# One fold over n and d before the split into even and odd, a fifth halved step in some blocks, and a first load in four pieces

## The chip, the cores and the metric

The kernel runs on one core of one Trainium2 chip. The metric is the device time of one execution in microseconds (us). TensorE (PE) multiplies matrices, PEld is its weight load, VectorE (DVE), ScalarE (ACT) and GpSimd (POOL) work elementwise, and SyncE (SP) only issues transfers here. POOL issues the loads, the transfers through the scratch tensor and the spread copies; SP issues the stores of the output.

## The reference

The input x is (8, 3008, 256), w_in (256, 2048), w_out (2048, 256), all float32.

```python
X = np.fft.fft(x, axis=1)
X = np.fft.fft(X, axis=2)
a = X.real.reshape(8 * 3008, 256)
h = np.maximum(a @ w_in, 0.0)
out = h * h @ w_out
```

Only the real part of the transform is used, so row k of a batch and row -k are linked, and x can be folded: what is needed of it are sums and differences of x(n,d), x(-n,-d), x(n,-d) and x(-n,d).

## The kernel before

**Transform.** The transform over d is multiplied into w_in once: `gh` holds three matrices (128 x 2048), cosine, sine, and -2 times the sine (`gh_turn`). The transform over n is done by TensorE on folded data. Per batch i, `load_x` loads x as fp16 into `t`, four quarters of six rows for each of 128 partitions: quarters 0 and 1 straight (`direct`), quarters 2 and 3 mirrored in n (`mirrored`, an indirect gather). There is one buffer for it, so the next load waits for the last reader of this one. `fold_steps(i)` then folds it on DVE:

- `d_even` (L389) sums d with -d into `fe`, `d_odd` (L396) takes their difference into `fo`, for all four quarters (24 rows of 128). `d_odd` also issues the next load of x.
- `n_cos` (L402) and `n_sin` (L405) combine a quarter with its mirrored one into `ab` (cosine and sine part, 12 rows of 130 each).
- `odds` (L412, or `odd` for one part) gives `od` for the odd rows of the output, `nyq` fills in its column 0 by two tiny matmuls, `even` (L422) gives `ev`, which goes to DRAM and comes back differently laid out (`back`) for the late fold (`late`: fold8, fold16, nyq8) of the even rows.
- `z_steps` multiplies `od` (unit (i, 0)) or the late fold's tiles (unit (i, 1)) with tables of cosines and sines; ACT evicts the first half of such a sum to `es` (L531) and the second to the columns zc, zs; DVE adds the mirrored half of the columns (`minus`, L542). Part 0 is zc, part 1 zs, and h is the half.

**Blocks.** The output columns are worked off in 25 blocks w (`wins`; widths 240, 512, 376, 376, 512, 448, then 512 and a last one of 360). A block goes through eight steps s of 256 hidden units each. A full step makes p+q by four matmuls into a PSUM tile `ph` (`pq`), lets ACT evict it with ReLU and DVE or ACT square it (`square`; steps in the second list of the plan have the first square done by ACT), turns it into p-q by two more (`turn`), and evicts and squares again. A halved step (`half_q`, `half_p`) makes q by two matmuls, evicts -2q to `sn` (L822), adds p by two more, evicts p+q to `hd` (L830), and leaves p-q, the ReLU and the square to DVE (`row_sum`: L838, L842; `halves`: L852, L853, L854), for one or two steps at a time. So a halved step has four ph matmuls where a full one has six, and more DVE work. `plan(w)` says which steps are halved; `PLAN` holds the lists.

Between the halves of each step `others(s)` puts the work of other kinds into the queues: the jobs `at[s]` of the folds, two of the 16 parts of the previous block's second matmul (L669, eight matmuls of 256 columns each, evicted by L684 and stored), the jobs `post[s]`, and from step `lo` on the z matmuls for the next block. The order of each engine's queue is the order in which this code runs (manual schedule). Both h2 (the squares) and `hd` have two buffers, h1 five, `ph` two. `row_spread` has POOL copy row 0 of zs to all partitions (`eb`) for L838.

Blocks by what they do besides: with the first part of a fold (`first_at`: 4, 7, 9, 11, 14, 17; d_even and n_cos), with its main part (`fold_at`: 5, 8, 10, 13, 16, 19; d_odd, n_sin, odds, nyq, even, back), with the late fold (`late_at`: 6, 9, 12, 15, 18, 21). Block 1 has the whole fold 1, block 2 the table for the even rows. Halved steps by block from 5 on: 4 5 5 4 3 4 5 5 4 5 5 4 5 5 4 6 5 6 6 5.

**Start.** Tables of cosines are made while x is loaded; `fold_steps(0)` runs by quarters (L578 to L590), then the first z matmuls, with `gh` made in between: `gh_step` (L475, both parts of 512 columns, one scaled by ACT, one by DVE) and `gh_half` (L486, one part, scaled by DVE). Block 0 has its own order (L891 to L917), four hidden chunks at a time (`pq4`, `turn4`, `square4`), with the last parts of `gh` between. `idle` issues matmuls whose result nobody reads.

## Time and profile before

| | |
|---|---|
| time, median of 3 runs | 595.66 us (595.61 to 595.82) |
| the profiled execution, its own time | 595.68 us |
| its span | 593.90 us |
| granted clock of TensorE | 1.00 |
| start to the first matmul of block 0 | 19.5 us |
| blocks 0 to 4 | 19.5 to 110.9 us |
| blocks 5 to 23 | 110.9 to 558.6 us |
| block 24 and the last second matmul | 558.6 to 593.9 us |

A busy share is the mean over all these stretches. Matmul rows overlap each other, so their busy time is an upper bound of what TensorE needs; the distance from one start to the next tells the pace. An arrow `<-` in a bracket names what ended the idle time before a row. First matmuls of some blocks (us from the start of the span): block 1 at 28.11, 2 at 48.43, 4 at 88.11, 5 at 110.88, 8 at 179.93, 9 at 203.56, 10 at 228.51, 11 at 252.55, 12 at 276.74, 13 at 299.66, 14 at 323.89.

### The profile page before, as it was taken

The page shows a single profiled execution, that of the slowest core. Times are in us where ns is not written, and L with a number is a line of the kernel's source. Part 1 is how long each engine was busy: PE and PEld are TensorE (multiplying, and loading weights), DVE is VectorE, ACT ScalarE, POOL GpSimd, SP SyncE. Part 2 cuts the span into 40 slices and gives each one's busy share as a digit, 9 for nine tenths or more (in the row PEclk, how much of TensorE's full clock was granted, in tenths as well). Part 3 has the DMA queues.
Part 4 walks back from the last instruction along what each step waited for, and adds up shares of the span by engine and source line. Part 5 has one row for each costly group of instructions (what it writes and reads, how often), then busy time and mean ns, then how long its engine had stood idle before and what let it go on. Part 6 is the DMA issues. An engine that isn't in the chain of part 4 may idle for free.

```text
span 593.9 us, 11346 instructions
## 1 busy us (share of the span) xinstructions
PE 574.7 (97%) x4352; PEld 418.4 (70%) x4352; DVE 533.8 (90%) x777; ACT 515.4 (87%) x665; POOL 109.9 (18%) x153
## 2 busy tenths in 40 slices
...
GB/s 147 206 119 138 54 87 36 80 132 102 51 56 106 120 87 86 118 114 59 40 116 104 111 41 46 115 125 92 49 36 68 70 100 43 53 51 46 63 58 68
DMA packets 37630, 50.42 MB, mean 85 GB/s; under 512 B 4583, under 2 KB 30743, under 8 KB 37575
## 3 DMA queue, kind: packets, MB, share of 16 engines
...
q1 hardware_dynamic: 26899, 24.44, 13.7%
q8 instruction: 34, 0.56, 0.4%
...
q14 instruction: 21, 0.17, 0.1%
...
## 4 chain that ended last, share of the span: by engine, by line
PE 66%; ACT 16%; DVE 9%; issue 6%; DMA 1%; ACTq 0%; POOL 0%; SPq 0%; DVEq 0%; POOLq 0%
PE po L669 39%; PE ph L828 7%; ACT h L799 7%; PE ph L814 6%; PE ph L789 4%; PE ph L790 4%; PE ph L795 4%; PE pz L526 3%; ACT sn L822 3%; ACT osb L684 2%; ACT hd L830 2%; DMA xo<-in_x_dram 1%; DVE hd L852 1%; ACT h L802 1%; DVE hd L853 1%
## 5 line engine op out<-in xcount | busy, mean ns | idle before, releaser
L669 PE MATMUL po<-wout,h 128*128 128x256 f16 (+1 forms) x3024 | 361.7, 273 | 0.0
L669 PEld LDWEIGHTS <-h 128*128 128x128 f16 (+1 forms) x3024 | 296.6, 98 | 71.2
L799 ACT ACTIVATE h<-ph 128x1024 f16<-128x1024 f32 (+3 forms) x172 | 164.3, 990 | 5.7 <-PE ph L790 3.3
L830 ACT ACTIVATE hd<-ph 128x1024 f16<-128x1024 f32 (+3 forms) x106 | 104.8, 990 | 26.2 <-PE ph L828 21.8
L854 DVE TENSOR_TENSOR h<-hd 128x4096 f16<-128x4096 f16 (+6 forms) x59 | 117.7, 1995 | 2.5
L822 ACT ACTIVATE sn<-ph 128x1024 f16<-128x1024 f32 (+3 forms) x106 | 104.6, 988 | 0.6 <-PE ph L814 0.6
L842 DVE TENSOR_TENSOR sn<-sn,hd 128x2048 f16<-128x2048 f16 (+6 forms) x59 | 63.5, 1076 | 16.3 <-ACT sn L822 12.0
L804 DVE TENSOR_TENSOR h<-h 128x1024 f16<-128x1024 f16 (+3 forms) x108 | 68.4, 668 | 8.6 <-ACT h L799 8.0
L852 DVE TENSOR_TENSOR hd<-hd,sn 128x2048 f16<-128x2048 f16 (+6 forms) x59 | 63.4, 1074 | 7.3 <-ACT hd L830 5.4
L684 ACT ACTIVATE osb<-po 128x512 f32<-128x512 f32 (+3 forms) x95 | 54.4, 576 | 15.7 <-PE po L669 14.9
L802 ACT ACTIVATE h<-h 128x1024 f16<-128x1024 f16 (+3 forms) x64 | 65.0, 1015 | 2.0
L828 PE MATMUL ph<-zc,gh 128*128 128x512 f16 (+3 forms) x212 | 61.0, 369 | 4.8 <-ACT sn L822 4.3
L853 DVE TENSOR_SCALAR hd<-hd 128x4096 f16<-128x4096 f16 (+6 forms) x59 | 63.7, 1080 | 1.6
L789 PE MATMUL ph<-zc,gh 128*128 128x512 f16 (+3 forms) x172 | 63.7, 371 | 0.6 <-ACT h L885 0.3
L790 PE MATMUL ph<-zs,gh 128*128 128x512 f16 (+3 forms) x172 | 63.7, 371 | 0.0
L838 DVE TENSOR_SCALAR hd<-eb,wv 128x512 f16<-128x512 f16 (+3 forms) x212 | 61.4, 346 | 2.5 <-DMA eb<-zs 2.5
L814 PE MATMUL ph<-zs,gh 128*128 128x512 f16 (+3 forms) x212 | 61.0, 370 | 0.0
L795 PE MATMUL ph<-zs,gh 128*128 128x512 f16 (+3 forms) x172 | 48.8, 370 | 0.2
...
L814 PEld LDWEIGHTS <-gh 128*128 128x128 f16 x212 | 20.6, 97 | 23.1
L790 PEld LDWEIGHTS <-gh 128*128 128x128 f16 x172 | 16.8, 98 | 19.0 <-issue 1.0
L789 PEld LDWEIGHTS <-gh 128*128 128x128 f16 x172 | 16.7, 97 | 18.1
...
## 6 DMA issues: line engine op xcount, KB each, us to landing
...
```

The lines of the kernel that those rows point to most:

```text
L669: nc.tensor.matmul(po[0:m, j * D : (j + 1) * D], h2[:, fc, q : q + m], wout16[:, fc, :], start=(fc == 0 and (j == 0 or not four or i > 3)) ...
L789: nc.tensor.matmul(ph[:, a, 0:wn], gh[:, 0, f0 : f0 + P], zcw[:, 0:wn], start=True, stop=False)
L790: nc.tensor.matmul(ph[:, a, 0:wn], gh[:, 1, f0 : f0 + P], zsw[:, 0:wn], start=False, stop=True)
L795: nc.tensor.matmul(phs[s][:, a, 0:wn], gh[:, 2, f0 : f0 + P], zsw[:, 0:wn], start=False, stop=True, skip_group_check=True)
L799: nc.scalar.activation(h1[:, :, 0:wn], phs[s][:, :, 0:wn], AF.Relu)
L802: nc.scalar.activation(h2[:, 2 * s : 2 * s + 2, 0:wn], hv, AF.Square)
L814: nc.tensor.matmul(ph[:, a, 0:wn], gh[:, 1, f0 : f0 + P], zsw[:, 0:wn], start=True, stop=True)
L822: nc.scalar.activation(sns[g][:, i : i + 2, 0:wn], ph[:, :, 0:wn], AF.Copy, bias=0.0, scale=-2.0)
L828: nc.tensor.matmul(ph[:, a, 0:wn], gh[:, 0, f0 : f0 + P], zcw[:, 0:wn], start=False, stop=True, skip_group_check=True)
L830: nc.scalar.activation(hds[g][:, i : i + 2, 0:wn], ph[:, :, 0:wn], AF.Copy, bias=0.0, scale=1.0)
L853: lambda: nc.vector.tensor_scalar(out=hv, in0=hv, scalar1=0.0, scalar2=None, op0=ALU.max),
L854: lambda: nc.vector.tensor_tensor(h2[:, 2 * g[0] : 2 * g[-1] + 2, 0 : 2 * wn], hv, hv, op=ALU.mult),
```

## The change

The fold starts with one sum over both signs, `cs` = x(n,d) + x(-n,-d) (`sums`, 12 rows of 255, column 0 apart into `ab`), from which `even_d` and `odd_d` make the cosine and sine part of `ab` by adding or subtracting the mirrored d (12 rows of 128). `fe` and `fo` go, `ab` is made once. The first part of a fold is now `sums` and `even_d`, the main part `load`, `odd_d` and the rest as before; block 1 has sums, then even_d and load, then odd_d.

The plan: main-fold blocks (5, 8, 10, 13, 16, 19) halve five steps (0 1, 3 4, 6) in place of four (1 2, 4 5); block 9 halves four in place of three; the others stay.

The first load comes as quarter 0, quarter 2, quarter 1, quarter 3, and the first fold works on quarters 0 and 2, then 1 and 3. `gh_step` is folded into `gh_half`; in block 0 the scalings of `gh` come ahead of the squares, whose DVE half `square4` now returns; `even` of fold 0 moves from block 0's step 7 to before block 0. In block 4 the z matmuls of unit (1,1) go part 0, part 1, part 0, part 1.

```diff
@@ -60,8 +60,8 @@
     PLAN = {
         6: (((0, 1), (2, 3), (4, 5)), (6, 7)),
         5: (((0, 1), (2, 3), (4,)), (5, 6, 7)),
+        "main": (((0, 1), (3, 4), (6,)), (2, 5, 7)),
         4: (((1, 2), (4, 5)), (0, 3, 6)),
-        3: (((1, 2), (4,)), (0, 5, 6)),
         "third": (((2, 3), (4, 5)), (0, 1, 6, 7)),
         "fourth": (((1, 2), (3, 4), (5,)), (0, 6, 7)),
         "fifth": (((2, 3),), ()),
@@ -146,10 +146,11 @@
         def mirrored(q):
             gather(q, idx["r" if q == 3 or b + 1 < B else "c"][:, 0:1], o + ((S if q == 2 else H) - R * (P - 1)) * D)
 
-        if b > 0:
+        if i == 0:
+            direct(0, 1)
+            yield t
+        elif b > 0:
             direct(0, 2)
-            if i == 0:
-                yield t
         else:
 
             gather(0, idx["f"][:, 0:1], o + D)
@@ -157,6 +158,8 @@
             direct(1, 2)
 
         mirrored(2)
+        if i == 0:
+            direct(1, 2)
         if b + 1 == B:
 
             nc.gpsimd.dma_start(
@@ -290,11 +293,10 @@
 
     spn = fop.tile([P, 2, 2, P], F16, name="spn")
     nc.vector.memset(spn, 0.0)
-    fe = fop.tile([P, 4, R, 130], F16, name="fe")
-    fo = fop.tile([P, 4, R, 130], F16, name="fo")
-    fo0 = fo.rearrange("p q c d -> p (q c) d")[:, :, 0:1]
-    nc.vector.memset(bass.AP(tensor=fo0.tensor, offset=fo0.offset, ap=list(fo0.ap[0:2]) + [[129, 2]]), 0.0)
-    nc.vector.memset(fe.rearrange("p q c d -> p (q c) d")[:, :, 129:130], 0.0)
+    cs = fop.tile([P, 2, R, D], F16, name="cs")
+    ab = fop.tile([P, 2, 2, R, 130], F16, name="ab")
+    nc.vector.memset(ab[:, 1, :, :, 0:1], 0.0)
+    nc.vector.memset(ab[:, :, :, :, 129:130], 0.0)
     turn2 = small([P, 1], "turn2")
     nc.vector.tensor_scalar(out=turn2, in0=dvec, scalar1=0.0, scalar2=2.0, op0=ALU.is_equal, op1=ALU.mult)
     nc.vector.tensor_scalar(out=turn2, in0=turn2, scalar1=-2.0, scalar2=None, op0=ALU.add)
@@ -377,33 +379,27 @@
 
     def fold_steps(i):
         t = xs.pop(i)
-        ab = fop.tile([P, 2, 2, R, 130], F16, name="ab", tag="ab")
         od = evp.tile([P, 2, R, 130], F16, name="od", tag="od")
         ev = fop.tile([P, R, 2, 130], F16, name="ev", tag="ev")
         folded[i, 0] = od
         st = {}
-        xf = t.rearrange("p q c d -> p (q c) d")
-        fef = fe.rearrange("p q c d -> p (q c) d")
-        fof = fo.rearrange("p q c d -> p (q c) d")
-
-        def d_even(a=0, b=4, eng=nc.vector):
-            r = slice(R * a, R * b)
-            if a < 3 <= b:
+
+        def sums(a=0, b=2, eng=nc.vector):
+            if a == 0:
                 nc.vector.tensor_copy(t[0:1, 2, 0, :], t[0:1, 0, R - 1, :])
-            eng.tensor_copy(fef[:, r, 0:1], xf[:, r, 0:1])
-            nc.vector.tensor_tensor(fef[:, r, 1:129], xf[:, r, 1:129], rev_dim(xf[:, r, 128:256], 2), op=ALU.add)
-
-        def d_odd(a=0, b=4):
-            r = slice(R * a, R * b)
-            nc.vector.tensor_tensor(fof[:, r, 1:129], xf[:, r, 1:129], rev_dim(xf[:, r, 128:256], 2), op=ALU.subtract)
-            if i + 1 < B and b == 4:
+            m = t[:, a + 2 : b + 2]
+            nc.vector.tensor_tensor(cs[:, a:b, :, 1:D], t[:, a:b, :, 1:D], rev_dim(rev_dim(m[:, :, :, 1:D], 2), 3), op=ALU.add)
+            eng.tensor_tensor(ab[:, 0, a:b, :, 0:1], t[:, a:b, :, 0:1], rev_dim(m[:, :, :, 0:1], 2), op=ALU.add)
+
+        def load():
+            if i + 1 < B:
                 xs[i + 1] = next(load_x(i + 1))
 
-        def n_cos(a=0, b=2):
-            nc.vector.tensor_tensor(ab[:, 0, a:b], fe[:, a:b], rev_dim(fe[:, a + 2 : b + 2], 2), op=ALU.add)
-
-        def n_sin(a=0, b=2):
-            nc.vector.tensor_tensor(ab[:, 1, a:b], fo[:, a:b], rev_dim(fo[:, a + 2 : b + 2], 2), op=ALU.subtract)
+        def even_d(a=0, b=2):
+            nc.vector.tensor_tensor(ab[:, 0, a:b, :, 1:129], cs[:, a:b, :, 1:129], rev_dim(cs[:, a:b, :, 128:256], 3), op=ALU.add)
+
+        def odd_d(a=0, b=2):
+            nc.vector.tensor_tensor(ab[:, 1, a:b, :, 1:129], cs[:, a:b, :, 1:129], rev_dim(cs[:, a:b, :, 128:256], 3), op=ALU.subtract)
 
         def odd(part):
 
@@ -468,28 +464,27 @@
             nc.gpsimd.tensor_copy(spn[:, 1, :, 0:1], yt[:, 0, 0, :, 128:129])
 
         late = [lambda: fold8(0), lambda: fold8(1), lambda: fold16(0), lambda: (fold16(1), nyq8())]
-        return {"d_even": d_even, "n_cos": n_cos, "odd": odd, "odds": odds, "d_odd": d_odd, "n_sin": n_sin, "nyq": nyq, "even": even, "back": back, "late": late}
+        return {"sums": sums, "load": load, "even_d": even_d, "odd_d": odd_d, "odd": odd, "odds": odds, "nyq": nyq, "even": even, "back": back, "late": late}
 
     gh = const.tile([P, 3, F], F16, name="gh")
 
-    def gh_step(cc):
+    def gh_half(cc, i, act=False):
         f0 = cc * 512
         fw = f0 % (F // 2)
-        pg = ps_h.tile([P, 2, 512], F32, name="pg", tag="psh")
-        for i, t in enumerate((c_all, s_n)):
-            for c in range(2):
-                nc.tensor.matmul(pg[:, i, :], t[:, c, 0:P], w16[f0 // (F // 2)][:, c, fw : fw + 512], start=(c == 0), stop=(c == 1))
-        nc.scalar.activation(gh[:, 0, f0 : f0 + 512], pg[:, 0, :], AF.Copy, bias=0.0, scale=1.0 / HS)
-        nc.vector.tensor_scalar(out=gh[:, 1, f0 : f0 + 512], in0=pg[:, 1, :], scalar1=1.0 / HS, scalar2=None, op0=ALU.mult)
-        gh_turn(cc)
-
-    def gh_half(cc, i):
-        f0 = cc * 512
-        fw = f0 % (F // 2)
-        pg = ps_o.tile([P, 512], F32, name="pg", tag="po")
+        if act:
+            pg = ps_h.tile([P, 2, 512], F32, name="pg", tag="psh")[:, 0, :]
+        else:
+            pg = ps_o.tile([P, 512], F32, name="pg", tag="po")
         for c in range(2):
             nc.tensor.matmul(pg, (c_all, s_n)[i][:, c, 0:P], w16[f0 // (F // 2)][:, c, fw : fw + 512], start=(c == 0), stop=(c == 1))
-        return lambda: nc.vector.tensor_scalar(out=gh[:, i, f0 : f0 + 512], in0=pg, scalar1=1.0 / HS, scalar2=None, op0=ALU.mult)
+
+        def scale():
+            if act:
+                nc.scalar.activation(gh[:, i, f0 : f0 + 512], pg, AF.Copy, bias=0.0, scale=1.0 / HS)
+            else:
+                nc.vector.tensor_scalar(out=gh[:, i, f0 : f0 + 512], in0=pg, scalar1=1.0 / HS, scalar2=None, op0=ALU.mult)
+
+        return scale
 
     def gh_turn(cc):
         f0 = cc * 512
@@ -575,29 +570,27 @@
 
     f0s = fold_steps(0)
     z0 = z_steps(need[0][0], late=True)
-    f0s["d_even"](0, 2, nc.gpsimd)
-    f0s["d_odd"](0, 2)
-    f0s["d_even"](2, 3, nc.gpsimd)
+    f0s["sums"](0, 1, nc.gpsimd)
+    f0s["even_d"](0, 1)
     nc.gpsimd.dma_start(out=wout16, in_=moe_w_out.rearrange("(c p) o -> p c o", p=P))
-    f0s["n_cos"](0, 1)
-    f0s["d_odd"](2, 3)
-    f0s["n_sin"](0, 1)
-    f0s["d_even"](3, 4, nc.gpsimd)
-    f0s["n_cos"](1, 2)
+    f0s["odd_d"](0, 1)
+    f0s["sums"](1, 2, nc.gpsimd)
+    f0s["load"]()
+    f0s["even_d"](1, 2)
     f0s["odd"](0)
-    f0s["d_odd"](3, 4)
-    f0s["n_sin"](1, 2)
+    f0s["odd_d"](1, 2)
     f0s["odd"](1)
     run(*z0(0, 0))
     idle(3)
     run(*z0(0, 1))
     f0s["nyq"]()
-    gh_step(0)
-    run(*z0(1, 0))
-    gh_step(1)
-    run(*z0(1, 1))
+    for h in range(2):
+        run(gh_half(h, 0, True), gh_half(h, 1))
+        gh_turn(h)
+        run(*z0(1, h))
     gh_half(2, 0)()
     run(*z0(0, 2), *z0(1, 2))
+    f0s["even"]()
     evec_i = iota([P, 2], [[1, 2]], 0, 2, "evec_i")
 
     evec = small([P, 2], "evec")
@@ -705,7 +698,7 @@
 
     def fold_jobs(i):
         f = folds[i] = fold_steps(i)
-        return [f["d_even"], f["n_cos"], f["d_odd"], f["n_sin"], f["odds"], f["nyq"], f["even"], f["back"]]
+        return [f["sums"], f["even_d"], f["load"], f["odd_d"], f["odds"], f["nyq"], f["even"], f["back"]]
 
     fold_at, late_at = {}, {}
     for i in range(2, B):
@@ -725,10 +718,11 @@
         if w < 5:
             return PLAN[("third", "fourth", "fifth")[w - 2]]
         first, late, main = w in first_at, w in late_at, w in fold_at
-        if w == 6 or late and not need[w + 1]:
-            return PLAN[5]
-        n = 4 if main or late else 5 if first or w + 1 == NW else 6
-        return PLAN[n - (first and late)]
+        if first and late:
+            return PLAN[4]
+        if main:
+            return PLAN["main"]
+        return PLAN[5 if first or late or w + 1 == NW else 6]
 
     def halved(w):
 
@@ -746,7 +740,7 @@
         at = [[] for _ in range(NST)]
         post = [[] for _ in range(NST)]
         if w == 0:
-            at[7] = [f0s["even"], f0s["back"]]
+            at[7] = [f0s["back"]]
         elif w == 1:
             fj = fold_jobs(1)
             at = [fj[0:1], fj[1:3], fj[3:4], fj[4:5], [], [], [], []]
@@ -778,7 +772,7 @@
         zj, zl = [], []
         for u in need[w + 1]:
             zu = z_steps(u)
-            zj += [(zu, p, h) for p, h in (((0, 0), (1, 0), (1, 1), (0, 1)) if lo == 4 else ((1, 0), (0, 0), (1, 1), (0, 1)))]
+            zj += [(zu, p, h) for p, h in (((0, 0), (1, 0), (0, 1), (1, 1)) if lo == 4 else ((1, 0), (0, 0), (1, 1), (0, 1)))]
         f2 = ffn2_steps(*old) if old else []
         phs = {}
 
@@ -885,32 +879,27 @@
             nc.scalar.activation(h1[:, :, 0 : 2 * wn], phs[s][:, :, 0 : 2 * wn], AF.Relu)
             hv = h1[:, :, 0 : 2 * wn].rearrange("p a (b n) -> p a b n", b=2)
             hv = rev_dim(hv, 3) if sg else hv
-            nc.vector.tensor_tensor(h2[:, 2 * s : 2 * s + 4, sg * wn : (sg + 1) * wn].rearrange("p (a b) n -> p a b n", b=2), hv, hv, op=ALU.mult)
+            return lambda: nc.vector.tensor_tensor(h2[:, 2 * s : 2 * s + 4, sg * wn : (sg + 1) * wn].rearrange("p (a b) n -> p a b n", b=2), hv, hv, op=ALU.mult)
 
         ng = 2 if w == 0 or wins[w - 1][1] < 384 < wn else 1
         if w == 0:
             pq4(0)
-            gh_half(2, 1)()
             pq4(2)
-            square4(0, 0)
-            gh_turn(2)
-            square4(2, 0)
+            g2 = gh_half(2, 1)
+            p0, p2 = square4(0, 0), square4(2, 0)
             turn4(0)
-            gh3 = [gh_half(3, 0)]
+            g3 = [gh_half(3, 0)]
             turn4(2)
-            gh3.append(gh_half(3, 1))
-            run(*gh3)
-            square4(0, 1)
-            square4(2, 1)
-            gh_turn(3)
+            g3.append(gh_half(3, 1))
+            m0, m2 = square4(0, 1), square4(2, 1)
+            run(g2, *g3, p0, lambda: gh_turn(2), p2, lambda: gh_turn(3), m0, m2)
             for s in (4, 6):
                 pq4(s)
-            for s in (4, 6):
-                square4(s, 0)
-            for s in (4, 6):
-                turn4(s)
-            for s in (4, 6):
-                square4(s, 1)
+            for sg in range(2):
+                for s in (4, 6):
+                    if sg:
+                        turn4(s)
+                run(*[square4(s, sg) for s in (4, 6)])
             for s in range(NST):
                 others(s)
             old = (w, h2)
```

## The prediction

> **What bounds the kernel now.** I read the page's busy times first, then the timeline for the pace of TensorE, then the busy time by stretch, one stretch per column block, and last the DVE rows of the fold and the places where TensorE waits.
>
> ```profile
> PE 574.7 (97%) x4352; PEld 418.4 (70%) x4352; DVE 533.8 (90%) x777; ACT 515.4 (87%) x665; POOL 109.9 (18%) x153
> ```
>
> Three engines are nearly full, so a share alone decides nothing. The pace of TensorE is the distance between starts, since a row's own length is pipelined:
>
> ```profile
> 40.84 0.96 DVE L413 TENSOR_TENSOR od<-ab 128x1548 f16<-128x1548 f16 x1
> ...
> 41.86 0.18 PE L418 MATMUL py<-od,perm 128*128 128x1 f16 x1 [0.39 <-DVE od L413]
> ...
> 41.93 0.38 PE L789 MATMUL ph<-zc,gh 128*128 128x512 f16 x1
> ...
> 42.14 0.38 PE L790 MATMUL ph<-zs,gh 128*128 128x512 f16 x1
> ...
> 42.36 0.38 PE L789 MATMUL ph<-zc,gh 128*128 128x512 f16 x1
> ```
>
> A 512-column matmul follows the one before after 0.215 us. The chain of waits has sixteen 256-column ones of L669 in 1.75 us, 0.109 each. Block 13 (299.66 to 323.89) holds 128 of these (14.0), 40 of 512 columns (8.6) and 1.2 us of small z matmuls: 23.8 of its 24.23 us. The same count over blocks 5 to 23 (110.9 to 558.6) leaves only some 9 us of 448 in which TensorE lacks work. So a matmul taken out of a block is worth its 0.215 us, as long as DVE and ACT can follow. How near they are:
>
> ```profile
> 179.93:203.56 23.63, 23.16 (x172) 16.46 (x170) 22.03 (x28) 21.00 (x25) 3.37 (x4) 1.00 0.61 119
> 203.56:228.51 24.95, 24.95 (x184) 17.79 (x183) 22.65 (x37) 22.24 (x28) 5.91 (x10) 1.00 0.43 81
> 252.55:276.74 24.19, 24.19 (x179) 17.41 (x178) 23.29 (x34) 21.64 (x29) 6.41 (x6) 1.00 0.47 95
> 276.74:299.66 22.92, 22.42 (x167) 16.21 (x166) 21.75 (x32) 20.30 (x24) 3.67 (x5) 1.00 0.30 42
> 299.66:323.89 24.23, 24.16 (x191) 17.76 (x190) 22.28 (x27) 22.73 (x31) 5.45 (x5) 1.00 0.65 124
> ```
>
> Each line is a block: its length, then busy PE, weight load, DVE, ACT, POOL; the clock is 1.00. The last three are one period (fold's first part, late fold, main fold). In it DVE works 67.3 of 71.3 us, ACT 64.7.
>
> **Part 1, the fold's arithmetic on DVE.**
>
> ```profile
> L394 DVE TENSOR_TENSOR fe<-xo 128x3072 f16<-128x3072 f16 x7 | 12.4, 1779 | 0.0
> L398 DVE TENSOR_TENSOR fo<-xo 128x3072 f16<-128x3072 f16 x7 | 12.4, 1778 | 0.0
> ...
> L403 DVE TENSOR_TENSOR ab<-fe 128x1560 f16<-128x1560 f16 x7 | 6.7, 963 | 0.0
> L406 DVE TENSOR_TENSOR ab<-fo 128x1560 f16<-128x1560 f16 x7 | 6.7, 963 | 0.0
> ```
>
> 3072 and 1560 elements give 0.54 ns an element and about 0.13 us fixed. Removed per fold: 1.78+1.78+0.96+0.96 and the 0.22 us copy of L393, 5.70. Added: the sum of 12 rows of 255, 3060 elements, 1.77; its column 0 (12 elements, from the 0.22 of the copy); even and odd part, 1536 elements each, 0.96 twice. Together 3.91, so 1.8 us less DVE work. It falls unevenly: the first part (L394+copy+L403, 2.96) is 2.95 after, the main block's (L398+L406, 2.74) becomes 0.96. What no row shows is a reversed operand with rows of odd length: L413 has odd rows (12 of 129, 966 ns for 1548), L394 reversed rows. Bounds for the sum: 1.5 us, L394 less its fixed part and a little, and 3.4 us, if it ran at the pace of L542 (546 ns for 376 elements, 255 for 102: 1.06 ns each). I take 1.77: it is nearest to L394 in everything but the one element. The Trainium skill (VectorE: DVE Perf Modes, Mode 2×_1P) asks for 4-byte alignment for two elements a cycle, and the sum starts at element 1, two bytes past; by that it would take the upper bound, and the time would be that of the half-pace rival below. L394 starts at element 1 too and has the fast pace, so the trace speaks against the rule here.
>
> **Part 2, a fifth halved step.** The rule for the plan changes seven blocks by one step: 5, 8, 10, 13, 16 and 19 from four halved steps to five, 9 from three to four. A full step has six ph matmuls, a halved one four: two fewer, 6 x 0.431 us and, for block 5 with 448 columns (0.188 each), 0.38: **-2.96 us** of TensorE. ACT keeps two evictions a step and three squares a block: no change. DVE per main block: a single halved group adds two rows of L838 (0.35 each), 0.69 of L842, 0.69 of L852, 0.69 of L853, 1.23 of L854, 4.0; two squares of L804 (0.68 each) go: +2.6, and part 1 gives back 1.8. Net +0.8, and some 0.65 with the overlap of neighbouring rows. Block 9 has no gain from part 1: a pair (7.4) replaces a single (4.0), two squares go, +2.0.
> The cover: DVE idles 1.95 us in block 13 and 1.6 in block 8; after, TensorE needs 23.3 and 22.2 us there and DVE some 23.0 and 22.7. The 0.5 us that block 8 lacks can stand over, since h2 has two buffers and its later half is read only in step 2 of the next block, some 5 us in; block 10 has 2 us to spare. If that cover fails, late DVE work holds up the buffers of ACT and then TensorE (below). ACT is the nearer trouble: 22.7 us in block 13 against 23.3. TensorE already waits there 0.2 us twice, and up to 0.67 in block 12, for the eviction L822, on which the second half of a halved step depends. One more such step per block gives 0 to 0.4 us more of this: 0 if ACT's own idle time (1.5 us in block 13) covers it, 0.4 from the two 0.2 us waits that a pair has now. I take 0.15 for each of six blocks: **+0.9**.
>
> **Part 3, the start.**
>
> ```profile
> 8.41 0.98 DVE L394 TENSOR_TENSOR fe<-xo 128x1536 f16<-128x1536 f16 x1 [0.66 <-DMA xo<-in_x_dram]
> ...
> 13.44 0.57 DVE L403 TENSOR_TENSOR ab<-fe 128x780 f16<-128x780 f16 x1
> 14.04 0.57 DVE L410 TENSOR_TENSOR od<-ab 128x774 f16<-128x774 f16 x1
> ...
> 14.67 0.65 PE L526 MATMUL pz<-cos,od 128*128 128x376 f16 x3 [1.60 <-DVE od L410]
> ```
>
> TensorE waits for od, the last of ten DVE operations that begin with the data at 8.41. The landings in the trace: first two quarters 8.39, third 10.20, fourth 12.06; the queue streams about 105 KB in 0.5 us without a break, so cutting the first load in two and putting the third quarter between its halves moves no total: quarters 0 and 2 at about 8.4, quarter 1 at about 10, quarter 3 at 12.06. The first pair's operations (0.2+1.0+0.6+0.6) end by 10.9. The second sum starts at 12.08, +1.0, the even part +0.6, od +0.57: 14.28 in place of 14.61, **-0.33**. The issues behind on POOL's queue (both halves of w_in, w_out) move by one load's issue, 0.6 us at most; w_in's first half landed at 15.6 and is wanted at 16.1, so it holds. POOL's small column operation is bounded by 0.2 (L611) and 0.9 (L467), and must be done by 13.7; it may start at 12.1, so it is hidden, and 0.2 us late at worst.
> In block 0 the evictions of gh move ahead of the squares, and the even sum of fold 0 (L424, 0.97) from the end of the block to its front. TensorE's wait for gh (0.5 at 25.30) and for h1 (0.8 at 27.25) are both DVE lateness. Laid out by the rows, the third quarter of gh is scaled by 22.6, the last by 24.0 in place of 25.24, and the first matmul of block 1 comes at about 27.1 in place of 28.11, 0.33 of it already counted: **-0.7** (bounds: +0.5, if the early even sum delays the first squares of which ACT wants the buffers, and -1.3, both waits). In block 1 the wait at 41.86 (0.39 on od, 0.56 with the pipeline) goes, DVE being 1.8 us earlier: **-0.56**.
>
> **Part 4, order of z in block 4.**
>
> ```profile
> 104.55 0.49 ACT L531 ACTIVATE es<-pz 128x377 f32<-128x377 f32 x1
> ...
> 105.08 0.24 PE L526 MATMUL pz<-sin,xt 128*128 128x188 f16 x1 [0.57 <-ACT es L531]
> ```
>
> The second half of part 1 follows its first half at once and waits for the eviction. With part 0 between, that wait goes: **-0.57** (bounds 0 and -0.74, the whole gap between starts). zs is then finished last, about 109.9; block 5 wants it in its first matmuls at 110.3 and its spread copy at step 1 instead of 2. POOL's copy landing later there would delay only L838 on DVE, which has 3.5 us idle in block 5.
> The load of the next x moves ahead of the odd part; POOL's issue then waits for the sum, done a block earlier: its three issues come up to 9.7 us sooner (POOL's wait for L398 in the period shown), and what is queued behind them on POOL, the copies of zs and the store of ev, waits no longer than now. No cost.
>
> **Sum.** The profiled execution took 595.68 (span 593.90, 1.78 around it; median of the runs 595.66). -2.96+0.9-0.33-0.7-0.56-0.57 = -4.2: **591.5 us**.
>
> **Rivals.** *ACT takes the place of TensorE* in the main blocks and the fifth step buys nothing: only the first 110 us gain, 2.2, so 593.5. For it: ACT at 94% of block 13 and every steady wait of TensorE being for L822. Against: block 9 runs with 0.04 us lost while ACT is 89% busy.
> *DVE becomes the bound* (the other side). Its idle time of 1.95 us in a main block may be waits that cannot be squeezed; then each main block grows by DVE's net +0.7, block 9 by 2.0: 6.2 in all, less 2.2 at the start, 599.7. It decides from the point where a main block cannot run with less than 0.8 us of DVE idle. Against: blocks 11 and 4 run with 0.9 and 0.4.
> *The sum runs at half pace*: +1.6 us a fold, DVE 69.6 of a period for which TensorE needs 69.5. With 2.6 us of idle left (4.0 now) a period takes 72.2 instead of 71.3, five times, +4.5, less the 2.2 at the start: 598.
> *The divided load doesn't do what it says*: its pieces land a microsecond later for the added issue, and od is 0.7 later than now instead of 0.33 earlier: 592.5.
>
> **How the numbers follow.** Chances: forecast 0.63 (own range 590.2 to 593.0), ACT 0.17, load 0.05, DVE bound 0.10, half pace 0.05. A measurement here can tell about 0.2%, 1.2 us. Faster by more: the first and nearly all of the second and third, 0.82; within: their rest and the milder ends of the slow ones, 0.06; slower 0.12. The range 590.0 to 595.0 takes in no give-back and both start waits gone at its lower end, and the ACT rival with the start half lost at its upper.
>
> **What would show it.** The sum of 3060 elements near 1.77 us; od's first matmul near 14.3; block 1 starting near 27.1; no wait before the z matmul near 104; block 13 at about 23.95, the waits on the sn eviction within 0.65 us, ACT 22.7 and DVE 23. The forecast is wrong if DVE rows leave no idle in main blocks and TensorE waits grow past 0.43 each, or if the sum takes 3 us.

## The result: 597.74 us against 595.66, and the profile after

The changed kernel is slower: a median of 597.74 us (597.10 to 598.71, seven runs) against 595.66 (595.52 to 595.82, seven runs), ratio 1.0036 with a 95% interval of 1.0024 to 1.0048. The profiled execution took 598.18 us with a span of 596.40, 2.50 more than the span before. The starts of the blocks' first matmuls say where these 2.50 us are:

| stretch | before | after | difference | predicted |
|---|---|---|---|---|
| start to block 0 | 19.53 | 23.35 | +3.82 | -0.33 |
| blocks 0 to 4 | 91.35 | 89.14 | -2.21 | -1.83 |
| blocks 5 to 23 | 447.69 | 448.73 | +1.04 | -2.06 |
| block 24 and the end | 35.33 | 35.18 | -0.15 | 0 |

So there are two misses, at the start and in the main blocks, and blocks 0 to 4 came out 0.38 us better than predicted. Of the +1.04, 0.28 lie in block 23, whose plan is unchanged; that part is not explained. First the page's busy times and its row of the granted clock, one digit for each fortieth of the span:

```profile
PE 573.8 (96%) x4338; PEld 417.8 (70%) x4338; DVE 534.4 (90%) x790; ACT 514.2 (86%) x665; POOL 120.8 (20%) x153
...
PEclk9899999999999999999999999999999999999999
```

TensorE has 14 matmuls fewer, as counted, and the second slice (14.9 to 29.8 us) ran at a reduced clock, where the mean over the whole span was 1.00 before. The timeline of the start shows the rest (start, length, engine, line; the bracket has the idle time of the engine and what ended it):

```profile
10.85 0.21 DVE L389 COPY xo<-xo 1x256 f16<-1x256 f16 x1 [2.79 <-DMA xo<-in_x_dram,idx_r]
11.10 0.96 DVE L391 TENSOR_TENSOR cs<-xo 128x1530 f16<-128x1530 f16 x1
...
14.64 0.96 DVE L391 TENSOR_TENSOR cs<-xo 128x1530 f16<-128x1530 f16 x1 [1.51 <-DMA xo<-in_x_dram,idx_r]
14.70 0.99 POOL L392 TENSOR_TENSOR ab<-xo 128x6 f16<-128x6 f16 x1 [1.42 <-DMA xo<-in_x_dram,idx_r]
...
16.31 0.57 DVE L406 TENSOR_TENSOR od<-ab 128x774 f16<-128x774 f16 x1
16.94 0.65 PE L521 MATMUL pz<-cos,od 128*128 128x376 f16 x3 [4.01 <-DVE od L406]
...
19.15 1.01 PE L479 MATMUL pg<-w,c_all 128*128 128x512 f16 x2
...
22.01 0.59 PE L479 MATMUL pg<-w,s_n 128*128 128x512 f16 x2
```

DVE's first sum had to wait for a gathered quarter until 10.85 and its second until 14.64, where the prediction had the data at 8.4 and 12.06. od's first matmul comes at 16.94 in place of 14.67, TensorE stands idle for 4.01 us before it, and after that a pair of 512-column matmuls takes 1.01 us at 19.15 and a like pair 0.59 at 22.01. The busy time by stretch has the clock for it (start and end, length, then busy PE, weight load, DVE, ACT, POOL, the granted clock, DMA share and GB/s), and beside it the blocks that answer to those shown of before:

```profile
17.97:21.38 3.41, 3.33 (x12) 1.36 (x11) 0.51 (x2) 1.28 (x4) 1.24 (x2) 0.50 1.42 198
181.15:204.74 23.59, 22.70 (x169) 16.34 (x168) 22.18 (x30) 20.59 (x24) 0.00 (x0) 1.00 0.45 107
204.74:229.26 24.52, 24.52 (x181) 17.61 (x180) 23.14 (x35) 22.42 (x29) 4.87 (x8) 1.00 0.45 83
253.46:277.70 24.24, 24.24 (x180) 17.40 (x178) 23.62 (x33) 21.95 (x30) 5.65 (x6) 1.00 0.46 93
277.70:300.62 22.92, 22.41 (x167) 16.21 (x166) 21.41 (x32) 20.31 (x24) 6.60 (x7) 1.00 0.31 44
300.62:325.27 24.65, 23.86 (x190) 17.63 (x189) 22.35 (x32) 22.26 (x30) 2.54 (x3) 1.00 0.71 121
```

For 3.41 us the clock was half; by estimate that costs about half of that, 1.7 us. Of the blocks, 9 (second to be shown, 204.74) lost 0.43 us as counted, from 24.95 to 24.52; 8 stayed (23.63, 23.59); 13, the last, became longer, from 24.23 to 24.65, although it has two matmuls fewer. Counted by the pace of the rows (0.215 and 0.109 us a matmul), TensorE's need in block 13 fell from 23.76 to 23.33, and the time in which it lacks work rose from 0.47 to 1.31. DVE and ACT are no busier than predicted (22.35 for 23, 22.26 for 22.7). Where the 1.31 lie is seen at an entry, a halved step that follows a full one; ACT's and TensorE's timeline at the third of the block's three, step 5 to 6:

```profile
318.90 0.58 ACT L677 ACTIVATE osb<-po 128x512 f32<-128x512 f32 x1
319.38 0.54 ACT L530 ACTIVATE zc<-pz 128x300 f16<-128x300 f32 x2
319.80 1.03 ACT L793 ACTIVATE h<-ph 128x1024 f16<-128x1024 f32 x1
320.70 1.05 ACT L816 ACTIVATE sn<-ph 128x1024 f16<-128x1024 f32 x1
```

```profile
319.27 0.38 PE L808 MATMUL ph<-zs,gh 128*128 128x512 f16 x1
319.48 1.91 PE L662 MATMUL po<-wout,h 128*128 128x256 f16 x16
321.23 0.17 PE L414 MATMUL py<-od,perm 128*128 128x1 f16 x1
321.80 0.59 PE L822 MATMUL ph<-zc,gh 128*128 128x512 f16 x2 [0.37 <-ACT sn L816]
```

The second half of the halved step (L822) needs the eviction sn (L816; L822 in the kernel before), and that stands in ACT's queue behind the last ReLU of the full step, an output eviction and two z evictions. TensorE has only sixteen second matmuls to go on with, 1.75 us, and then waits: 0.51 us against its pace. The other two entries of the block cost 0.45 (step 7 to 0) and 0.29 (2 to 3). Before, with steps 1 2 and 4 5 halved, there were two entries of 0.18 and 0.22. The first of them, step 0 to 1, in the timeline of before (there L822 is the eviction sn and L828 the second half of the step; the two z matmuls at 305.14 are done at their pace by 305.22, and L828 starts at 305.40, when L822 has ended):

```profile
304.33 1.01 ACT L822 ACTIVATE sn<-ph 128x1024 f16<-128x1024 f32 x1
305.14 0.25 PE L526 MATMUL pz<-cos,spn 128*128 128x94 f16 x2
305.40 0.59 PE L828 MATMUL ph<-zc,gh 128*128 128x512 f16 x2
```

What came out as predicted: the operations of the fold, in the groups of DVE by form (calls, then busy us and mean ns of one, then idle before them).

```profile
L391 DVE TENSOR_TENSOR cs<-xo 128x3060 f16<-128x3060 f16 x7 | 12.3, 1764 | 0.2
L402 DVE TENSOR_TENSOR ab<-cs 128x1536 f16<-128x1536 f16 x7 | 6.8, 967 | 0.0
L399 DVE TENSOR_TENSOR ab<-cs 128x1536 f16<-128x1536 f16 x7 | 6.8, 967 | 0.0
L392 DVE TENSOR_TENSOR ab<-xo 128x12 f16<-128x12 f16 x7 | 1.4, 201 | 0.0
```

The sum of 3060 elements takes 1764 ns (1.77 predicted), the pace of the sums of before (3072 elements in 1779 ns).

### The profile page after: what moved, and what is told of

It is laid out like the page before. It is cut to its first block, busy times and chain, and to the rows that moved or that the text cites. A ratio compares the mean times of both kernels' runs of the same rounds, so it can differ in the third digit from the quotient of the medians.

```text
span 596.4 us, 11364 instructions
## 1 busy us (share of the span) xinstructions
PE 573.8 (96%) x4338; PEld 417.8 (70%) x4338; DVE 534.4 (90%) x790; ACT 514.2 (86%) x665; POOL 120.8 (20%) x153
## 4 chain that ended last, share of the span: by engine, by line
PE 39%; DVE 22%; ACT 20%; issue 10%; DMA 4%; SPq 3%; POOL 1%; ACTq 0%; DVEq 0%; POOLq 0%
PE po L662 22%; ACT h L793 8%; PE ph L822 5%; DVE h L848 5%; ACT sn L816 4%; DVE hd L846 4%; PE ph L808 4%; DVE sn L836 4%; DVE hd L847 3%; SPq L641 3%; DVE hd L832 3%; ACT hd L824 3%; PE pz L521 2%; ACT osb L677 2%; DMA out_dram<-osb 2%
## 5 line engine op out<-in xcount | busy, mean ns | idle before, releaser
L793 ACT ACTIVATE h<-ph 128x1024 f16<-128x1024 f32 (+3 forms) x158 | 151.4, 988 | 3.4 <-PE ph L784 2.0
L824 ACT ACTIVATE hd<-ph 128x1024 f16<-128x1024 f32 (+3 forms) x113 | 111.9, 991 | 34.5 <-PE ph L822 30.0
L848 DVE TENSOR_TENSOR h<-hd 128x4096 f16<-128x4096 f16 (+7 forms) x65 | 126.0, 1938 | 3.2
L816 ACT ACTIVATE sn<-ph 128x1024 f16<-128x1024 f32 (+3 forms) x113 | 111.8, 990 | 0.6 <-PE ph L808 0.6
L836 DVE TENSOR_TENSOR sn<-sn,hd 128x2048 f16<-128x2048 f16 (+7 forms) x65 | 68.1, 1048 | 15.6 <-ACT sn L816 11.0
L822 PE MATMUL ph<-zc,gh 128*128 128x512 f16 (+3 forms) x226 | 65.1, 369 | 8.1 <-ACT sn L816 7.5
L846 DVE TENSOR_TENSOR hd<-hd,sn 128x2048 f16<-128x2048 f16 (+7 forms) x65 | 67.8, 1043 | 5.3 <-ACT hd L824 2.9
L847 DVE TENSOR_SCALAR hd<-hd 128x4096 f16<-128x4096 f16 (+7 forms) x65 | 68.4, 1052 | 1.9
L808 PE MATMUL ph<-zs,gh 128*128 128x512 f16 (+3 forms) x226 | 65.1, 370 | 0.0
L798 DVE TENSOR_TENSOR h<-h 128x1024 f16<-128x1024 f16 (+3 forms) x94 | 59.8, 668 | 4.4 <-ACT h L793 4.0
L784 PE MATMUL ph<-zs,gh 128*128 128x512 f16 (+3 forms) x158 | 58.5, 370 | 0.0
L789 PE MATMUL ph<-zs,gh 128*128 128x512 f16 (+3 forms) x158 | 44.7, 370 | 0.2
L808 PEld LDWEIGHTS <-gh 128*128 128x128 f16 x226 | 21.9, 97 | 24.6
L822 PEld LDWEIGHTS <-gh 128*128 128x128 f16 x226 | 20.7, 97 | 17.3 <-issue 12.0
L784 PEld LDWEIGHTS <-gh 128*128 128x128 f16 x158 | 15.4, 97 | 17.5 <-issue 1.0
```

The lines of the kernel that those rows point to most:

```text
L784: nc.tensor.matmul(ph[:, a, 0:wn], gh[:, 1, f0 : f0 + P], zsw[:, 0:wn], start=False, stop=True)
L793: nc.scalar.activation(h1[:, :, 0:wn], phs[s][:, :, 0:wn], AF.Relu)
L808: nc.tensor.matmul(ph[:, a, 0:wn], gh[:, 1, f0 : f0 + P], zsw[:, 0:wn], start=True, stop=True)
L816: nc.scalar.activation(sns[g][:, i : i + 2, 0:wn], ph[:, :, 0:wn], AF.Copy, bias=0.0, scale=-2.0)
L822: nc.tensor.matmul(ph[:, a, 0:wn], gh[:, 0, f0 : f0 + P], zcw[:, 0:wn], start=False, stop=True, skip_group_check=True)
L824: nc.scalar.activation(hds[g][:, i : i + 2, 0:wn], ph[:, :, 0:wn], AF.Copy, bias=0.0, scale=1.0)
```

## The experiments

Thirteen kernels ran. "e1" to "e13" are the numbers in the labels; each edit is against the kernel named. Block 0 is the start of its first matmul, blocks 13 and 14 are lengths.

| run | us, median | ratio to before (95%) | block 0 at | block 13 | block 14 |
|---|---|---|---|---|---|
| before | 595.66 | 1 | 19.53 | 24.23 | 24.19 |
| after | 597.74 | 1.0036 (1.0024 to 1.0048) | 23.35 | 24.65 | 24.24 |
| e1 first load as before | 594.17 | 0.9971 (0.9955 to 0.9987) | 19.60 | 24.65 | 24.25 |
| e4 busy wait | 596.07 | 1.0006 (0.9996 to 1.0015) | 21.16 | 24.64 | 24.24 |
| e8 cut only | 596.80 | 1.0018 (1.0008 to 1.0028) | 21.77 | 24.65 | 24.24 |
| e13 loads first | 595.76 (one run) | | 21.06 | 24.65 | 24.24 |
| e3 e1, plan as before | 593.76 | 0.9968 (0.9958 to 0.9978) | 19.66 | 24.23 | 24.19 |
| e2 e1, one entry | 600.33 | 1.0081 (1.0055 to 1.0107) | 19.62 | 23.60 | 26.23 |
| e5 e1, steps 0 to 4 | 597.56 | 1.0031 (1.0019 to 1.0043) | 19.50 | 25.42 | 24.24 |
| e6 e2, copy earlier | 597.47 | 1.0036 (1.0023 to 1.0049) | 19.62 | 24.74 | 24.23 |
| e7 three edits on e1 | 622.91 | 1.0450 (1.0436 to 1.0465) | 19.25 | 31.33 | 24.23 |
| e9 e1, two entries | 592.46 | 0.9942 (0.9925 to 0.9958) | 19.60 | 24.05 | 24.30 |
| e10 e1, late pair | 593.43 | 0.9961 (0.9951 to 0.9971) | 19.63 | 23.78 | 25.07 |
| e11 e3, odd later at the start | 593.27 | 0.9953 (0.9939 to 0.9967) | 19.28 | 24.25 | 24.19 |
| e12 e9, odd later at the start | 592.93 | 0.9954 (0.9940 to 0.9968) | 19.13 | 24.06 | 24.31 |

### The start: e1, e4, e8, e13

e1 takes the first load back to two quarters in one transfer, then the two gathered ones; everything else stays.

```diff
-        if i == 0:
-            direct(0, 1)
-            yield t
-        elif b > 0:
+        if b > 0:
             direct(0, 2)
+            if i == 0:
+                yield t
...
         mirrored(2)
-        if i == 0:
-            direct(1, 2)
```

> The changed kernel with the first load as before the change (quarters 0 and 1 in one transfer, then 2, then 3); all else changed. Theory (the divided load made the last quarter land 2.5 us later, TensorE then idled 4 us and ran 3.4 us at half clock): last quarter at 12.1 again, first od matmul at 14.3, clock 1.00 throughout, block 0 from 19.2 instead of 23.35, time 597.7-4.2 = 593.5. Rival (the new fold itself is slow to its first od, by the sum or by POOL's column operation): od's first matmul stays at 15.5 or later and the time stays above 595.5.

594.17 us, 3.6 less than after; the quarters landed at 8.34, 10.15 and 12.01 as before the change, the clock was 1.00 throughout. Block 0 starts at 19.60 in place of 23.35. So the divided load is 3.75 of the 4.15 us by which the start missed, and more than the whole slowdown. The timeline also shows why od's matmul, at 14.73, didn't get ahead of the 14.67 of before:

```profile
12.45 0.96 DVE L388 TENSOR_TENSOR cs<-xo 128x1530 f16<-128x1530 f16 x1
...
14.11 0.57 DVE L403 TENSOR_TENSOR od<-ab 128x774 f16<-128x774 f16 x1
14.73 0.65 PE L518 MATMUL pz<-cos,od 128*128 128x376 f16 x3 [1.66 <-DVE od L403]
```

The new fold's first sum needs the gathered quarter 2, so with this load DVE can't begin before 10.15 and reaches its second sum 0.4 us after the data. The block of the plan shows no change (busy time by stretch, block 13 of e1; compare the last row of after above):

```profile
296.88:321.53 24.65, 23.86 (x189) 17.63 (x188) 22.33 (x32) 22.26 (x30) 2.99 (x3) 1.00 0.73 123
```

e4 leaves the load divided and fills TensorE's wait with more of the matmuls whose result nobody reads:

```diff
-    idle(6)
+    idle(26)
```

> The changed kernel with 26 idle matmuls instead of 6 before the first od matmul, so that TensorE is busy while it waits for the load (3.2 us more of them, ending at about 16.2, before od at 16.9). Theory (of the 3.8 us lost at the start 2.3 are the late load and 1.5 the half clock that follows the idle 4 us): clock 1.00 throughout, od's first matmul still at 16.9, block 0 from 21.8 instead of 23.35, time 597.7-1.5 = 596.2. Rival (the clock costs nothing, as w_in and the evictions set the pace after od): block 0 from 23 or later, time 597.5.

```profile
11.79 4.39 PE L341 MATMUL pw<-spn 128*128 128x384 f16 x26
16.30 0.65 PE L521 MATMUL pz<-cos,od 128*128 128x376 f16 x3
...
18.05 0.59 PE L479 MATMUL pg<-w,c_all 128*128 128x512 f16 x2
```

In the timeline of e4 TensorE goes without a gap from the idle matmuls to od's, and the pair of 512 columns takes 0.59 us at once; the clock is 1.00 in the whole span. Block 0 starts 2.19 us earlier than after, 0.64 of it because od came earlier in this run (the last quarter landed at 13.91, not 14.55). The other 1.55 us are the price of the halved clock: from od's first matmul to block 0 it takes 4.86 us in e4, 4.87 in e1 and 6.41 in after.

e8 cuts the load but keeps the order 0, 1, 2, 3, so that a plain transfer, not a gather, comes second:

```diff
             direct(0, 1)
             yield t
+            direct(1, 2)
...
-        if i == 0:
-            direct(1, 2)
```

> The changed kernel with the first load in four transfers, but in the order quarter 0, 1, 2, 3. Theory (after the short first transfer the queue ran empty at 5.3 because a gather's data start some 2.5 us after its issue and a plain transfer's 1.2 us; with the plain second transfer in between it stays full): quarters land as before the change, the last at 12.1, od's first matmul at 14.7, clock 1.00, time as the run with the first load as before, 594. Rival (four transfers in place of three are the cost, whatever their order): the last quarter lands after 13 and block 0 starts after 21.

```profile
11.96 1.14 PE L340 MATMUL pw<-spn 128*128 128x384 f16 x6
15.74 1.12 PE L520 MATMUL pz<-cos,od 128*128 128x376 f16 x3 [2.65 <-DVE od L405]
```

```profile
15.26:18.67 3.41, 2.92 (x12) 1.46 (x13) 1.47 (x3) 0.48 (x1) 2.47 (x3) 0.50 1.22 204
```

The timeline and the busy time by stretch of e8: TensorE idles 2.65 us, and again 3.41 us at half clock follow. The last quarter landed at 13.03, about 1 us later than uncut, though no gather stood second. So the gather's place is not the whole cause.

e13 issues the four first transfers back to back, ahead of the index rows that POOL makes (IOTA):

```diff
             direct(0, 1)
-            yield t
...
+        if i == 0:
+            yield t
```

> The changed kernel with its four first transfers issued one behind the other on POOL, ahead of the index rows that stood between the first and the second; nothing left out. Only the landings are asked for, since the tables start some 3 us later. Theory (the first transfer is streamed out before the data of the second begin, because the second is issued too late): issued 0.7 us earlier, the second keeps the queue fed, the engines end within 0.6 us of one another and the last quarter lands at 12.1 to 12.4. Rival (a short transfer's descriptors reach the 16 engines unevenly whatever POOL does in between): single engines end 1 us or more behind the rest again and the last quarter lands at 13 or later.

One run: 595.76. The last pieces of the quarters, by the transfers' own records, and what the queue finished in half a microsecond between 5.5 and 7 us:

| | first to last quarter landed, us | KB in 0.5 us at 5.5 to 7 |
|---|---|---|
| before: 0 and 1 together, 2, 3 | 8.39, 10.20, 12.06 | about 105 |
| after: 0, 2, 1, 3 | 6.28, 10.75, 12.61, 14.55 | 49 at the lowest |
| e8: 0, 1, 2, 3 | (first not read), 9.30, 11.16, 13.03 | 43 to 61 |
| e13: 0, 2, 1, 3 back to back | 6.29, 9.54, 11.41, 13.35 | 31 to 46 |

With the issues back to back the queue has a hole as well, so POOL's other work between the issues isn't what makes it. That it adds to it is not shown: e4, with the same load as after, has the last quarter at 13.91, between e13 (13.35) and after (14.55).

The records of the single pieces show two forms of the loss. In e8 and e13 the queue isn't empty: nine of the 3 KB pieces that start at 5.3 to 6.1 us, just behind the first transfer, take 0.9 to 1.7 us each, where a piece takes 0.25 at that time in before, and most engines fall back. In after no piece that starts at 5 to 7 us takes over 0.7; there thirteen of the sixteen engines had ended their share of the last quarter by 12.04, as before, and three ran behind (12.86, 13.02, 14.55). So the engines end one transfer up to 3.5 us apart in after and 1.9 in e13, and within 0.9 in before. Why a short first transfer is followed by this is left open.

### The main blocks: e3, e2, e5, e6, e7, e9, e10

e3 is e1 with the plan of before, so what differs from before is the fold's arithmetic, the order of work at the start and in block 0, and the order of z in block 4:

```diff
-        "main": (((0, 1), (3, 4), (6,)), (2, 5, 7)),
+        "main": (((1, 2), (4, 5)), (0, 3, 6)),
+        3: (((1, 2), (4,)), (0, 5, 6)),
...
         if first and late:
-            return PLAN[4]
+            return PLAN[3]
```

> As e1, but with the plan of the kernel before (four halved steps in main-fold blocks, three in block 9): the new fold alone. Entry theory: two entries of 0.2 us again, blocks 13, 16, 19 at 24.2 as before the change, 0.4 under e1; block 9 0.4 and block 5 0.4 above e1; time e1 less 0.6, about 593. Rival (DVE holds the main blocks, so 1.8 us less DVE work shows there): blocks 13, 16, 19 well under 24.2, at 23.8 or less, time below 592.

```profile
297.55:321.78 24.23, 24.16 (x191) 17.75 (x190) 20.37 (x26) 22.73 (x31) 3.09 (x3) 1.00 0.70 124
```

593.76. In block 13 of e3 DVE has 20.37 us in place of 22.28, and the length is what it was, 24.23. The cheaper fold alone buys nothing there. The gain of e3, 1.9 us in the medians and 2.3 in the span, lies in blocks 0 (-0.95), 1 (-0.57) and 4 (-0.72), and the last of these comes with the order of z, not with the fold. And the five-step plan, worth -2.06 in the prediction, costs 0.4 in the medians (594.17 against 593.76) and 0.8 in the spans (592.4 against 591.6).

The seven blocks can halve five steps with fewer entries. e2 has one run of them with one entry:

```diff
-        "main": (((0, 1), (3, 4), (6,)), (2, 5, 7)),
+        "main": (((1, 2), (3, 4), (5,)), (0, 6, 7)),
```

> As e1, and the main-fold blocks halve steps (1 2)(3 4)(5) instead of (0 1)(3 4)(6): still five, but entered from a full step once per block and not three times. Theory (each entry, where ACT has the last ReLU of the full step, an output eviction and the sn eviction in a row, costs TensorE 0.3 to 0.5 us): blocks 13, 16 and 19 go from 24.65 to some 23.6, blocks 8 and 10 by some 0.7; time 4 to 5 us under e1, 589. Rival (a fifth halved step gives its gain back wherever it stands, because ACT and DVE are full): blocks 13, 16, 19 stay within 0.3 of 24.65, time as e1 within 1 us.

The time was 600.33 where 589 was expected. Block 13 went to 23.60, as the theory of entries has it, but the block behind it went from 24.25 to 26.23: a loss of two for a gain of one. The timeline of DVE and then of TensorE in block 14 of e2:

```profile
325.78 1.23 DVE L845 TENSOR_TENSOR h<-hd 128x2048 f16<-128x2048 f16 x1
326.93 0.96 DVE L417 TENSOR_TENSOR ev<-ab 128x1560 f16<-128x1560 f16 x1
327.81 0.18 DVE L413 CAST od<-py 128x6 f16<-128x6 f32 x1
```

```profile
328.04 0.49 PE L518 MATMUL pz<-sin,od 128*128 128x376 f16 x2 [1.87 <-DVE od L413]
```

The z matmuls wait for the copy of od's column 0, a row of 0.18 us that stands in DVE's queue behind the square of the late halved step (L845) and the even sum (L417).

e5 puts the five steps first, e6 takes e2 and puts that copy to the end of step 5, and e7 does both together with the start's edit of e11.

```diff
-        "main": (((0, 1), (3, 4), (6,)), (2, 5, 7)),
+        "main": (((0, 1), (2, 3), (4,)), (5, 6, 7)),
```

> First load as before; main-fold blocks halve (0 1)(2 3)(4): again five steps and one entry, but one step earlier than (1 2)(3 4)(5). The run with the latter had blocks 13, 16, 19 at 23.6 (1.05 less) while each following block lost 2.04 us at its first z matmul, which waited for column 0 of od, a DVE copy that stood behind the late halves. Theory (an entry costs TensorE 0.3 to 0.5, and DVE must be through with the halves early enough for the copy): main blocks near 23.6, the copy some 2.8 us earlier, the wait in the next block gone or under 0.5; time 594.2 less 4, 590. Rival (five consecutive halved steps cost the 2 us somewhere in any case, since DVE is the bound of the pair of blocks): blocks 13 and 14 together stay near 49.8, time 599 or more.

```diff
+        tail = [[] for _ in range(NST)]
...
-            post[6] = fj[5:6]
+            tail[5] = fj[5:6]
...
+            for j in tail[s]:
+                j()
```

> As the kernel with (1 2)(3 4)(5), only that the two tiny matmuls and the DVE copy that fill column 0 of od come at the end of step 5, behind the z matmuls, instead of in step 6; the work is the same. Theory (the 2.04 us in the block after a main block is the place of this copy in DVE's queue): the copy runs some 4 us earlier, the wait goes, block 14 back to 24.25, blocks 13 at 23.6; time 600.3 less 10, 590. Rival (DVE lags by 2 us there whatever stands in front): another wait of about 2 us takes its place in block 14, time 598 or more.

> The version that the two theories point to: first load as before, (0 1)(2 3)(4) in main-fold blocks, the copy into od at the end of step 5, and the first fold's order changed so that the odd part of the first quarters stands behind the first od. Expected: od's first matmul at 14.2 instead of 14.7 (0.5 less), main blocks 23.5, no wait at the next block's first z matmul; time 589.5. If DVE bounds the pair of blocks, 594 or more.

All three lose (597.56, 597.47 and 622.91 where 590, 590 and 589.5 were expected), each through the same kind of wait. TensorE's timelines of e5, e6 and e7, one line each:

```profile
319.77 0.16 PE L411 MATMUL py<-od,perm 128*128 128x1 f16 x1 [1.41 <-DVE zs L534]
```

```profile
317.95 0.16 PE L411 MATMUL py<-od,perm 128*128 128x1 f16 x1 [1.00 <-DVE zs L534]
```

```profile
249.33 0.16 PE L411 MATMUL py<-od,perm 128*128 128x1 f16 x1 [4.45 <-DVE zs L534]
```

The tiny matmul for the copy needs the PSUM buffer that zs's DVE operation (L534) still reads, and that operation is late behind the halves. In e6 moving the copy did take the wait of e2 away (block 14 is 24.23), and 1.14 of its 2 us came back here (block 13: 24.74 in place of 23.60). In e7 the wait has grown to 4.45 us (the row is of block 10, 30.86 us long), and the clock follows, as the busy time by stretch of e7 shows:

```profile
248.39:255.22 6.83, 5.89 (x24) 3.30 (x24) 5.42 (x9) 3.10 (x3) 0.57 (x1) 0.50 0.17 43
```

Block 13 of e7 is 31.33 us in the same way. The growth can be read from the two traces: in e5 and e7 alike zs's DVE operation starts 3.86 us after the last z matmul has ended (315.32 to 319.18, and 244.88 to 248.74), but in e5 TensorE has 3.04 us of a step's matmuls before the tiny one, and in e7, with the copy moved ahead, it has none: 1.41 + 3.04 = 4.45.

e9 and e10 have two entries each, with costs taken from the entries seen so far:

```diff
-        "main": (((0, 1), (3, 4), (6,)), (2, 5, 7)),
+        "main": (((0, 1), (2,), (4, 5)), (3, 6, 7)),
```

> First load as before; five halved steps in main-fold blocks as (0 1)(2)(4 5), so two entries from a full step (7 to 0, 3 to 4) as the kernel before had two, and a full step 3 in which DVE can catch up. Two theories that now stand together: each entry costs TensorE 0.2 to 0.5 us, and DVE must not fall so far behind that the z buffers or the copy into od are held. Expected: waits of 0.45 and 0.2, main blocks 13, 16, 19 at 24.0 (24.65 in the run with the first load as before, 24.23 with the old plan), time 592.5. If only DVE's sum counts, 24.65 as with (0 1)(3 4)(6), 594.2. If DVE lags at the end, a wait of 1 us or more for DVE at the two tiny matmuls or at the next z, time over 596.

```diff
-        "main": (((0, 1), (3, 4), (6,)), (2, 5, 7)),
+        "main": (((1, 2), (3,), (5, 6)), (0, 4, 7)),
```

> The same with (1 2)(3)(5 6): entries 0 to 1 and 4 to 5, behind steps in which no output eviction stands in front of the last ReLU, and the halves of the last pair behind the copy into od. Expected: waits 0.2 and 0.2, main blocks 23.8, time 590.5 if DVE's last pair, which ends some 2 us into the next block, holds up nothing there; otherwise the next block grows by what the main block gained, and the time is 594 or more.

```profile
296.55:320.60 24.05, 23.71 (x189) 17.54 (x188) 21.93 (x31) 22.30 (x30) 4.92 (x3) 1.00 0.66 124
320.60:344.90 24.30, 24.30 (x179) 17.31 (x178) 23.75 (x33) 22.01 (x30) 5.12 (x6) 1.00 0.44 89
```

```profile
295.99:319.77 23.78, 23.71 (x189) 17.57 (x188) 20.70 (x32) 22.41 (x30) 3.27 (x3) 1.00 0.73 123
319.77:344.84 25.07, 24.44 (x180) 17.39 (x178) 24.48 (x32) 21.95 (x30) 5.56 (x6) 1.00 0.44 87
```

Blocks 13 and 14, of e9 and then of e10. In e9 TensorE waits 0.45 (7 to 0) and 0.22 (3 to 4), in e10 0.18 (0 to 1) and 0.20 (4 to 5); in block 13 the same entry costs the same within 0.02 us in every kernel that has it, and both lengths of block 13 are within 0.05 us of what was forecast from them. In other blocks the price is another: counted in the same way, block 8 of after has entries of 0.67, 0.37 and 0.31, and block 9, with two entries, has no wait. In e10 the late pair moves DVE's work past the block's end (20.70 and 24.48 us of it in the two blocks, against 21.93 and 23.75 in e9), and block 14 loses 0.8 where a full step's turn waits for ACT behind late DVE work. e9 is the best kernel of the study: 592.46 (592.26 to 592.66), ratio 0.9942, ahead of the plan with four steps (e3) and of the one with three entries (e1). It loses 0.43 in block 6 against e1 (23.99 for 23.56), where the copy of od is late.

### Both together: e11, e12

e11 (on e3) and e12 (on e9) move the odd part of the first fold behind od, so that DVE reaches its second sum sooner:

```diff
     f0s["even_d"](0, 1)
...
-    f0s["odd_d"](0, 1)
...
     f0s["odd"](0)
-    f0s["odd_d"](1, 2)
+    f0s["odd_d"](0, 2)
```

> The new fold with the plan and the first load of the kernel before, and the odd part of the first quarters moved behind the first od. The run without this last move took 593.8. Expected: first od matmul at 14.4 instead of 14.7 and everything behind it 0.35 earlier: 593.4. If the first od was not what the start waited for, 593.8 as before.

> The two gains together: first load as before, (0 1)(2)(4 5) in main-fold blocks (592.5 by itself) and the odd part of the first quarters behind the first od (0.35 earlier in the run of the fold alone). They lie in different stretches, so they should add: 592.1, block 0 at 19.25, blocks 13, 16, 19 at 24.05. If the start's gain is taken back by later waits, 592.5.

e11 gave 593.27, 0.5 less than e3 in the medians and 0.25 in the spans, about as expected: what the change does beside the plan and the load is worth 2.4 us against before. e12 gave 592.93 where 592.1 was expected: block 0 starts 0.47 us earlier than in e9, and so does every block to the 20th, and then it is given back, 0.23 in block 21 and 0.65 in block 24. DVE's timelines of e12 and e9 in block 22, and then TensorE's of e12 in block 24:

```profile
514.82 1.14 DVE L828 TENSOR_SCALAR hd<-eb,wv 128x512 f16<-128x512 f16 x4 [1.17 <-DMA eb<-zs]
```

```profile
514.27 1.14 DVE L829 TENSOR_SCALAR hd<-eb,wv 128x512 f16<-128x512 f16 x4 [0.49 <-DMA eb<-zs]
```

```profile
560.94 0.83 PE L658 MATMUL po<-wout,h 128*128 128x256 f16 x6 [0.38 <-DVE h L844]
```

The spread copy of zs arrives 0.55 us later in a kernel that is 0.47 us ahead, and DVE waits 0.68 us more. DVE has next to no idle time in which to make it good: row for row it stays 0.53 us behind e9 up to block 24, where TensorE waits for its square (L844). That this is the cause of the 0.65 is read from the two traces; no run tested it. The 0.23 of block 21 come before it (TensorE waits at 505.92) and are not explained by it.

## Why the prediction was wrong

**The start, predicted -0.33, measured +3.82.** The step that failed is "cutting the first load in two and putting the third quarter between its halves moves no total". It took the queue's rate in a stream without breaks (105 KB in 0.5 us) as a rate that holds however the stream is cut. The cut alone costs about 1 us (e8, 13.03 for 12.06), back to back 1.3 (e13, 13.35), and the order chosen here 1.9 to 2.5 (13.91 in e4, 14.55 in after). The other 0.40 of the 4.15 us are the new fold's own: with the load as before its first sum waits for quarter 2 until 10.15, and od comes no earlier than before (e1). The rival of the divided load had this mechanism, but priced it at 1 us, put it down to the added issue, which e13 speaks against, and had no second step: the longer wait of TensorE is followed by 3.41 us at half clock, 1.55 us more by e4.

The Trainium skill (TensorE: Matmul & The Clock Gate, What's actually happening) says that the clock is gated to half by windows of 3.413 us, after an idle one, until a busy one. The lengths agree, 3.41 us here and in e8 and twice that, 6.83, in e7. In e7 the 3.41 us ahead of the first fall are idle, too (TensorE's wait is from 244.88 to 249.33, the clock falls at 248.39). But an idle window isn't needed: in e8 the 3.41 us ahead of the fall, 11.85 to 15.26, hold 1.14 us of matmuls whose result nobody reads, and the clock still fell. With a wait of 1.66 it didn't in the profiled execution of e1. But one of e1's seven runs has a clock of 0.997 and 1.76 us more than their median, about what 3.41 us at half clock would cost, and one of e8's eight has a clock of 1.00 and 1.53 us less. So the length of the wait alone doesn't decide it; what else does is open.

**The fifth step, predicted -2.96 + 0.9, measured +1.04 over blocks 5 to 23.** The matmuls went as counted, need in block 13 from 23.76 to 23.33. The failed step is the term of the give-back, "I take 0.15 for each of six blocks". The mechanism was named, the wait for the eviction sn, but it was sized by steps, and its unit is the entry from a full into a halved step: 0.2 to 0.5 us each in block 13, according to its place. The count of evictions ahead of sn in ACT's queue doesn't give the price by itself: with one besides the ReLU an entry cost 0.45 (step 7 to 0), with two 0.29 (2 to 3), with three 0.51 (5 to 6). Three entries in place of two took the time without work in block 13 from 0.47 to 1.31: +0.84, above even the upper bound of 0.4 (blocks 16 and 19 the same, 10 +0.58, 8 +0.39, 5 and 9 nothing). e9, with the same five steps and two entries, has 24.05, and 592.46 in place of 594.17. The upper bound itself was worked out from the two waits that "a pair has now"; they were among the cheapest entries that a block has.

**The rivals.** ACT in TensorE's place is the nearest in the main blocks, and as a sum it fell: ACT's busy time went down in block 13 (22.73 to 22.26), and what counts is its queue at three places. Its 593.5 is near what the change takes with the load as before (594.17), as the waits for sn, which were its evidence, are the ones that grew. That DVE becomes the bound came near the measured time (599.7) by another way: with 1.9 us less DVE work block 13 had the same length (e3), and in after DVE idles 2.3 us of it. But DVE decides where the halved steps can stand: late in the block they hold up the next one (e2, e10), together and early they hold up zs (e5, e7). The half-paced sum fell with the row of 1764 ns. The Trainium skill (VectorE: DVE Perf Modes, Mode 2×_1P) asks for 4-byte alignment for this pace; these operands start 2 bytes off, in rows of 255, one of them reversed in two dimensions, and the measurement decides against the rule.

**What held.** The fold's arithmetic, 1764, 967 and 201 ns for 1.77 us, 0.96 and about 0.2. Block 0 gained 0.90 (0.7 predicted), and the two waits behind DVE that were named for it, for gh (0.32) and for the square (0.65), are gone in after; block 1 gained 0.57 (0.56), and the order of z in block 4 gained 0.72 (0.57 taken, 0.74 the whole gap). Block 5 gained 0.49 (0.38 of it by matmuls), with the spread copy late in it, as said, without harm to TensorE; DVE's timeline there:

```profile
116.79 1.07 DVE L832 TENSOR_SCALAR hd<-eb,wv 128x448 f16<-128x448 f16 x4 [3.30 <-DMA eb<-zs]
```

POOL's column operation took 0.99 us, above its bound of 0.9, and was hidden.

**The sum.** -4.2 predicted, +2.50 of span measured. Of the 6.7 between them 4.15 are the start and 3.1 the main blocks; blocks 0 to 4 and the end came out 0.5 better.
